# A 128-column score stationary, a refitted plan, finer weight loads and a cut-up last chunk in a fused attention and feed-forward kernel

## The chip, the cores and the metric

The kernel runs on one core of a Trainium2 chip. The metric is the device time of one execution in microseconds (us), median over runs; lower is better. Ratios are computed as the mean time of one kernel's runs over the mean of the other's from the same rounds, so they are not quite the ratio of the medians that I quote.

Some words used throughout. TensorE (PE in the profiles) multiplies a *stationary* operand, which is loaded into it first (such a load is a PEld line), by a *moving* one that streams through it. A *span* is the time from the first to the last instruction of one profiled execution; the *granted clock* is the share of full speed that TensorE was given. A *spell* is a stretch at half clock. The *scores* are q times k, and AV (`ps_av`) is their exponential times v. *Dead* or *warm-up* matmuls are run for the clock alone; nobody uses their results.

## The reference

Cosine attention for 8 batches of 12 heads (448 tokens of 64), followed by a multiplicative feed-forward layer:

```
q_n = q / (norm(q) + 1e-6);  k_n = k / (norm(k) + 1e-6)
attn = softmax(q_n @ k_n.T / tau);  x = (attn @ v), heads side by side      # 3584 x 768
out = ((x @ w1) * (x @ w2)) @ w3 @ w_out                                     # 768 -> 1024 -> 768
```

The kernel forms W34 = w3 @ w_out once (16 units of work on TensorE at the start) and applies it in place of both; a "W34 group" is one such unit. Heads are handled in 48 pairs, which come in groups of three.

## The kernel before

The order of all work on the five engines is fixed at build time by a small planner. Each step has engines with costs (in us), a rank, predecessors and buffers. The planner simulates and emits in that order; each engine then works through its own queue in order.

```python
def earliest(self, name, eng):                    # when could this step start on this engine
    st, t = self.steps[name], self.free[eng]
    for a in st["after"]:
        t = max(t, self.end[a] + (self.HOP + st["slack"] if self.where[a] != eng else 0.0))
    ...
ready = {n for n, k in left.items() if k == 0}    # a set: ties are broken in an order that
...                                               # differs from build to build
```

The scores of a pair, two heads at a time in the two halves of the rows, four chunks of 112 keys:

```python
for t in range(2):                                # t = 0: q, t = 1: k
    for j in range(NJ):
        nc.tensor.transpose(ps[:, t, j * P:(j + 1) * P], ..., ident[:P, :P])
...
nc.tensor.matmul(sc[:P, hh, :S],
                 qks[pp][64 * hh:64 * hh + 64, 1, c * P:(c + 1) * P],   # stationary, P = 112
                 qks[pp][64 * hh:64 * hh + 64, 0, :],                   # moving, 448 columns
                 start=True, stop=True)
```

The preparation of q and k per pair is a square, a sum (VectorE), a root (ScalarE) and a scaling; from the third group on, squares and scalings are GpSimd's alone. v is copied into a tile with a column of ones by GpSimd (`v_sb`). Loads and the last chunk:

```python
w3_part = [slice(k, k + 2) for k in range(0, KO2, 2)]          # w_out in two halves of 384 columns
loads = ["q0", "k0", "w30", "wo0", "v0", "w31", "q1", "k1", "w32",
         "w33", "v1", "wo1", "q2", "k2", "w10", "v2", "w20"]   # q0, k0: heads 2 to 5 of the first group
...
# last chunk of the output: two groups of 384 columns, each copied and stored on its own
for n in range(60):
    add(f"warm{n}", [("PE", ...)], 10000 + n, lambda e: warm(), ..., until=11.0)   # dead matmuls
```

Of the kernel before, what the change touches and what calls it, by code (L numbers as in the profile page):

```python
# [8 lines left out]
FP32 = mybir.dt.float32  # L9
# [10 lines left out]
class Plan:  # L20
# [23 lines left out]
    def add(self, name, on, rank, emit, after=(), takes=(), holds=(), kb=0, later=None,  # L44
            until=None, slack=0.0, port=False):
        self.steps[name] = dict(on=on, rank=rank, emit=emit, after=list(after), later=later,
                                takes=list(takes), kb=kb, until=until, slack=slack, port=port)
        for key in holds:
            self.holders.setdefault(key, []).append(name)
# [9 lines left out]
    def earliest(self, name, eng):  # L59
        st, t = self.steps[name], self.free[eng]  # L60
        for a in st["after"]:
            t = max(t, self.end[a] + (self.HOP + st["slack"] if self.where[a] != eng else 0.0))
        if st["later"]:
# [16 lines left out]
    def order(self):  # L80
# [7 lines left out]
        left = {n: len(need) for n, need in needs.items()}  # L88
        ready = {n for n, k in left.items() if k == 0}
        self.lanes, ring = [], self.RING_FREE  # L90
        self.port = dict(DVE=0.0, POOL=0.0)
        out = []
        while ready:
# [12 lines left out]
            st = steps[n]  # L106
            out.append((t, len(out), n, eng))
            ready.discard(n)
            self.start[n], self.free[eng] = t, t + cost
# [9 lines left out]
            for u in users.get(n, ()):  # L119
                left[u] -= 1  # L120
                if left[u] == 0:
                    ready.add(u)
        late = [n for n, st in steps.items() if n not in self.end and st["until"] is None]
# [5 lines left out]
def kernel(  # L129
# [133 lines left out]
    def tr(pp):  # L263
        g, i = divmod(pp, GP)
        n = nrms[g]
        ps = psT.tile([128, 2, 512], BF16, tag="tr", name="ps_tr")
        for t in range(2):
            for j in range(NJ):
                nc.tensor.transpose(  # L269
                    ps[:, t, j * P:(j + 1) * P],  # L270
                    n[:, i, t, j].rearrange("p h d -> p (h d)"),
                    ident[:P, :P])
        qks[pp] = head_pool.tile([128, 2, S], BF16, tag="qkT", name="qkT")
        pst[pp] = ps
# [4 lines left out]
    def scores(pp, half):  # L279
        if half == 0:  # L280
            exps[pp] = exp_pool.tile([P, NJ, 2, S], BF16, tag="exp", name="expT")
        for c in (2 * half, 2 * half + 1):
            sc = psS.tile([128, 2, 512], FP32, tag="sc", name="sc")
            for hh in range(2):
                nc.tensor.matmul(  # L285
                    sc[:P, hh, :S],
                    qks[pp][64 * hh:64 * hh + 64, 1, c * P:(c + 1) * P],
                    qks[pp][64 * hh:64 * hh + 64, 0, :],
                    start=True, stop=True)
            scs[pp, c] = sc  # L290
# [63 lines left out]

    def w34(fo, mh):
        ps = pms["w34", fo, mh] = psM.tile([128, 512], FP32, tag="pm", name="ps_w34")
        mm_group([(w3t_sb[:, go, fo * 128:(fo + 1) * 128],
                   wo_sb[:, go, mh * NH:(mh + 1) * NH]) for go in range(KO2)], ps[:, :NH])

    def w34_copy(fo, mh, eng):  # L360
        copy(eng, w34_sb[:, fo, mh * NH:(mh + 1) * NH], pms.pop(("w34", fo, mh))[:, :NH])

# [36 lines left out]

    def out_group(bb, ch, mh):  # L400
        ps = pms["o", bb, ch, mh] = psM.tile([128, 512], FP32, tag="pm", name="ps_o")
        mm_group([(abts[bb][:, fo, ch * 128:(ch + 1) * 128],
                   w34_sb[:, fo, mh * NH:(mh + 1) * NH]) for fo in range(KO2)], ps[:, :NH])

    def out_copy(bb, ch, mh, eng):
        if mh == 0:
            osbs[bb, ch] = opool.tile([128, DM], FP32, tag="out_sb", name="out_sb")
        copy(eng, osbs[bb, ch][:, mh * NH:(mh + 1) * NH], pms.pop(("o", bb, ch, mh))[:, :NH])
        if (bb, ch) == (B // 2 - 1, 2 * S // 128 - 1):
            store(bb, ch, osbs[bb, ch], slice(mh * NH, (mh + 1) * NH),  # L410
                  (nc.sync, nc.scalar) if mh else (nc.sync,))
        elif mh == 1:
            store(bb, ch, osbs.pop((bb, ch)), slice(None), (nc.sync,))
# [18 lines left out]
    def ones():  # L432
        for t in v_tiles:
# [8 lines left out]

    add("ident", [("POOL", 0.6)], -90, lambda e: make_identity(nc, ident), later="w30")
    add("ones", [("POOL", 0.45)], -70, lambda e: ones())
    every = slice(None)
    w3_part = [slice(k, k + 2) for k in range(0, KO2, 2)]
    weights = dict(w10=(w1_sb, moe_w1, every, every), w20=(w2_sb, moe_w2, every, every),
                   wo0=(wo_sb, moe_w_out, every, slice(0, NH)),
                   wo1=(wo_sb, moe_w_out, every, slice(NH, DM)))
    for n, part in enumerate(w3_part):  # L450
        weights[f"w3{n}"] = (w3_sb, moe_w3, part, every)
    loads = ["q0", "k0", "w30", "wo0", "v0", "w31", "q1", "k1", "w32",
             "w33", "v1", "wo1", "q2", "k2", "w10", "v2", "w20"]
    for g in range(3, NG):
        loads += [f"q{g}", f"k{g}", f"v{g}"]
    before = None
    for name in loads:
# [34 lines left out]
    for g in range(NG):  # L492
        for i in range(GP):
            p = g * GP + i
            for t in range(2):
# [4 lines left out]
                else:  # L500
# [9 lines left out]
                    slack=0.6 if g > 2 else 0.0)  # L510
                add(f"scale{p}.{t}", [("POOL", 1.04)] if g else [("DVE", 0.62)], p - 2,
                    lambda e, g=g, i=i, t=t: prep_scale(g, i, t, engines[e]),
# [17 lines left out]
    for p in range(NP):  # L530
        g, i = divmod(p, GP)
        b, blk = divmod(p, NPAIR)
        last = p > 0
        add(f"tr{p}", [("PE", 0.42)], p - 1.2, lambda e, p=p: tr(p),
            [f"scale{p}.0", f"scale{p}.1", "ident"] + ([f"tr{p - 1}"] if last else []),
# [4 lines left out]
        for h in range(2):  # L540
            add(f"sc{p}.{h}", [("PE", 0.6)], p + 0.5 * h - 1, lambda e, p=p, h=h: scores(p, h),
                [f"ev{p}"] + ([f"sc{p}.0"] if h else [f"sc{p - 1}.1"] if last else []),
# [6 lines left out]
        for h in range(2):  # L549
            add(f"av{p}.{h}", [("PE", 0.53)], p + 0.5 * h, lambda e, p=p, h=h: av(p, h),  # L550
                [f"exp{p}.{c}" for c in range(NJ)] + [f"spread{g}"]
# [4 lines left out]
                lambda e, p=p, h=h: av_norm(p, h), [f"av{p}.{h}"], holds=[("av", p, h)])  # L556
        add(f"tb{p}", [("PE", 0.24)], p + 1, lambda e, p=p: trback(p),
            [f"an{p}.0", f"an{p}.1"] + ([f"tb{p - 1}"] if last else []),
# [3 lines left out]

    line = []

    def fill(nm, cost, em, after, on, em2, takes=(), holds=(), after2=(), holds2=()):
        add(nm, [("PE", cost)], 1000 + len(line), em, after, [("pm", ("pm", nm))] + list(takes),
            holds, later=line[-1] if line else None)
        add(nm + ".c", on, -50, em2, [nm] + list(after2), holds=[("pm", nm)] + list(holds2))
        line.append(nm)

    def add_w3t(fo):
        fill(f"w3t{fo}", 0.46, lambda e: w3t(fo), ["ident", f"w3{fo // 2}"],
             [("DVE", 0.62), ("ACT", 0.95)], lambda e: w3t_copy(fo, e), holds=[("w3_sb",)])

    def add_w34(fo, mh):
        fill(f"w34.{fo}.{mh}", 1.3, lambda e: w34(fo, mh), [f"wo{mh}", f"w3t{fo}.c"],
             [("DVE", 0.5), ("ACT", 0.45)], lambda e: w34_copy(fo, mh, e))

    add_w3t(0)
    add_w3t(1)  # L580
    for fo in range(KO2):
        add_w34(fo, 0)
        if fo + 2 < KO2:
            add_w3t(fo + 2)
    for fo in range(KO2):
        add_w34(fo, 1)
    for b in range(B):
        bb = b // 2
        def add_a(fo):
            fill(f"a{b}.{fo}", 1.14, lambda e, b=b: a_group(b, fo),  # L590
                 [f"xt{b * NPAIR + i}" for i in range(NPAIR)] + ["w10"], [("ACT", 0.46)],
                 lambda e, b=b: a_copy(b, fo), [("a_sb", ("a_sb", b, fo))], [("xT", b)])

        def add_b(fo):
            fill(f"b{b}.{fo}", 1.14, lambda e, b=b: b_group(b, fo),
                 ["w20"], [("DVE", 0.55)], lambda e, b=b: b_mul(b, fo),
# [11 lines left out]
        for ch in (range(0, 3) if b % 2 == 0 else range(3, 7)):  # L608
            for mh in range(2):
                fill(f"o{bb}.{ch}.{mh}", 1.3, lambda e, bb=bb, ch=ch, mh=mh: out_group(bb, ch, mh),  # L610
                     [f"b{b}.{fo}.c" for fo in range(KO2)] + [f"w34.{KO2 - 1}.1.c"],
                     [("DVE", 0.5), ("ACT", 0.45)],
                     lambda e, bb=bb, ch=ch, mh=mh: out_copy(bb, ch, mh, e),
                     [] if mh else [("out_sb", ("out_sb", bb, ch))], [("big", bb)],
                     holds2=[("out_sb", bb, ch)] if mh else [])
    for n in range(60):
# [41 lines left out]
```

## Time and profile before

| | before |
|---|---|
| median, first three runs | 405.77 us (405.07 to 406.02) |
| span of the profiled run | 403.9 us, clock 1.000 |
| TensorE (PE) busy | 392.7 us, 97% |
| ScalarE (ACT), GpSimd (POOL), VectorE (DVE) | 61%, 61%, 54% |

TensorE is the bound; the question for each part of a change is whether it takes TensorE time away or removes a wait in front of TensorE. The lines are in the prediction.

### The profile page before, as it was taken

Reading aid. Unit: us, or ns where it says so; the run is one execution under the profiler, and the core shown is the slowest. Engines: PE = TensorE matmul, PEld = TensorE weight load, DVE = VectorE, ACT = ScalarE, POOL = GpSimd, SP = SyncE. Lnnn points to the kernel's source line nnn. Section 1 sums busy time; section 2 is a strip of 40 time slices with the busy share of each in tenths; the row PEclk is TensorE's granted clock in tenths of the full one; section 3 lists DMA queues with packets and bytes.
Section 4 is the critical chain, followed back from the end, with each engine's and each line's share of the span. In section 5 each row is a group of like instructions: output and inputs, shape, how many; then the busy total and the mean of one; then the engine's idle time right before and its main releaser. Section 6 shows DMA issues by size and latency. Waiting matters only on the chain.

```text
span 403.9 us, 9389 instructions
## 1 busy us (share of the span) xinstructions
PE 392.7 (97%) x3944; PEld 233.5 (58%) x3944; DVE 217.9 (54%) x487; ACT 246.0 (61%) x396; POOL 245.9 (61%) x258
## 2 busy tenths in 40 slices
PE   8799999999999999999999999999999999999995
PEld 4466565556555565556565565656655566555553
DVE  5686546595575765758657658444345443420210
ACT  5786677657676666656667658656656656423222
POOL 8479799999999999999999998515100000000000
PEclk9999999999999999999999999999999999999999
DMA  8999999265683484841945282200210013003005
GB/s 154 200 206 207 210 198 137 36 79 74 149 102 47 59 151 111 104 57 16 171 84 69 26 156 80 36 2 2 80 39 2 2 41 108 12 0 107 12 6 153
DMA packets 42475, 35.18 MB, mean 87 GB/s; under 512 B 1856, under 2 KB 36416, under 8 KB 42432
## 3 DMA queue, kind: packets, MB, share of 16 engines
q0 software_dynamic: 37312, 23.11, 41.5%
q1 hardware_dynamic: 4752, 11.07, 9.3%
q8 instruction: 31, 0.51, 0.5%
q10 hardware_dynamic: 368, 0.40, 0.3%
q14 instruction: 12, 0.10, 0.1%
HBM read 46.66 MB, written 11.01 MB: 143 GB/s over the span
## 4 chain that ended last, share of the span: by engine, by line
PE 80%; POOL 12%; DMA 4%; issue 2%; DVE 1%; ACT 0%; POOLq 0%
PE ps_b L337 17%; PE ps_a L337 17%; PE ps_o L337 16%; PE ps_av L302 11%; PE sc L285 10%; POOL nrm L256 4%; PE ps_tr L269 4%; DMA raw<-in_k_dram 4%; POOL sq L230 3%; PE ps_w L337 3%; PE ps_tb L324 3%; POOL raw L199 1%; POOL v_sb L215 1%; POOL vraw L206 1%; POOL w_sb L218 1%
## 5 line engine op out<-in xcount | busy, mean ns | idle before, releaser
L293 ACT ACTIVATE expT<-sc 112x896 bf16<-112x896 f32 x192 | 165.6, 915 | 54.0 <-PE sc L285 54.0
L337 PEld LDWEIGHTS <-w_sb 128*128 128x128 bf16 x768 | 69.4, 98 | 56.5 <-issue 4.0
L256 POOL TENSOR_TENSOR nrm<-raw,rn 112x512 bf16<-112x512 bf16 x90 | 90.8, 1035 | 4.3 <-PE ps_tr L269 2.1
L230 POOL TENSOR_TENSOR sq<-raw 112x512 bf16<-112x512 bf16 x87 | 87.7, 1038 | 0.2
L337 PE MATMUL ps_b<-xT,w_sb 128*128 128x448 bf16 x384 | 83.0, 353 | 0.0
L337 PE MATMUL ps_a<-xT,w_sb 128*128 128x448 bf16 x384 | 82.9, 353 | 0.0
L337 PE MATMUL ps_o<-w_sb,abT 128*128 128x384 bf16 x448 | 80.1, 327 | 0.0
L302 PEld LDWEIGHTS <-expT 112*128 112x128 bf16 x1536 | 59.6, 98 | 20.6 <-issue 9.0
L236 DVE TENSOR_REDUCE ss<-sq 112x8 f32<-112x512 bf16 x96 | 63.7, 679 | 12.6 <-POOL sq L230 10.1
L383 DVE TENSOR_TENSOR abT<-a_sb,ps_b 128x448 bf16<-128x448 bf16 x64 | 39.6, 619 | 53.8 <-PE ps_b L337 52.6
L302 PE MATMUL ps_av<-v_sb,expT 112*128 112x65 bf16 x1536 | 65.6, 195 | 1.7 <-POOL v_sb L215 1.1
L372 ACT CAST a_sb<-ps_a 128x448 bf16<-128x448 f32 x64 | 34.1, 533 | 40.0 <-PE ps_a L337 39.4
L285 PE MATMUL sc<-qkT 64*112 64x448 bf16 x384 | 56.6, 372 | 0.4 <-ACT expT L293 0.4
L337 PEld LDWEIGHTS <-abT 128*128 128x128 bf16 x448 | 41.3, 98 | 26.8 <-issue 3.0
L343 ACT COPY out_sb<-ps_o 128x384 f32<-128x384 f32 x39 | 18.7, 478 | 39.3 <-PE ps_o L337 37.6
L315 DVE TENSOR_TENSOR osd<-ps_av,rs 128x256 bf16<-128x256 f32 x96 | 40.8, 425 | 3.3
L314 DVE RECIPROCAL rs<-ps_av 128x4 f32<-128x4 f32 x96 | 17.2, 179 | 46.5 <-PE ps_av L302 46.1
L215 POOL COPY v_sb<-vraw 112x1536 bf16<-112x1536 bf16 x16 | 23.4, 1462 | 23.0 <-PE ps_av L302 23.0
L277 DVE COPY qkT<-ps_tr 128x896 bf16<-128x896 bf16 x48 | 29.8, 620 | 13.5 <-PE ps_tr L269 13.4
L331 DVE COPY xT<-ps_tb 128x448 bf16<-128x448 bf16 x48 | 18.6, 387 | 22.3 <-PE ps_tb L324 22.3
L269 PE MATMUL ps_tr<-ident,nrm 112*128 112x112 bf16 x384 | 27.3, 213 | 2.7 <-DVE nrm L256 1.2
L285 PEld LDWEIGHTS <-qkT 64*112 64x112 bf16 x384 | 17.4, 125 | 20.9 <-issue 17.6
(37 smaller groups left out, 213.9 us busy)
## 6 DMA issues: line engine op xcount, KB each, us to landing
vraw<-in_v_dram POOLq DMA_DIRECT2D x16, 336.0 KB, 4.9
raw<-in_q_dram POOLq DMA_DIRECT2D x15, 336.0 KB, 5.1
raw<-in_k_dram POOLq DMA_DIRECT2D x15, 336.0 KB, 7.4
w_sb<-in_moe_w_dram POOLq DMA_DIRECT2D x2, 1536.0 KB, 25.1
out_dram<-out_sb SPq DMA_DIRECT2D x7, 336.0 KB, 2.8
out_dram<-out_sb SPq DMA_DIRECT2D x8, 288.0 KB, 3.1
w_sb<-in_moe_w_dram POOLq DMA_DIRECT2D x4, 512.0 KB, 15.5
out_dram<-out_sb SPq DMA_DIRECT2D x8, 240.0 KB, 2.8
```

What stands on the lines that cost most here:

```text
L230: eng.tensor_mul(o, x, x)
L236: nc.vector.reduce_sum(sss[g][:, t, 2 * i:2 * i + 2, :], sqs.pop((g, i, t)), axis=AX.X)
L256: eng.tensor_mul(nrms[g][:, i, t].rearrange("p j h d -> p h j d"), raw_of(g, t, i), rns[g][:, t, 2 * i:2 * i + 2].to_broadcast([P, 2, NJ, D]))
L269: nc.tensor.transpose(ps[:, t, j * P:(j + 1) * P], n[:, i, t, j].rearrange("p h d -> p (h d)"), ident[:P, :P])
L277: nc.vector.tensor_copy(qks[pp], pst.pop(pp)[:, :, :S])
L285: nc.tensor.matmul(sc[:P, hh, :S], qks[pp][64 * hh:64 * hh + 64, 1, c * P:(c + 1) * P], qks[pp][64 * hh:64 * hh + 64, 0, :], start=True, s ...
L293: nc.scalar.activation(exps[pp][:, c], scs.pop((pp, c))[:P, :, :S], ACT.Exp, scale=1.0 / float(tau))
L302: nc.tensor.matmul(ps[:, m, :], exps[pp][:, c, hh, q0:q0 + 128], vt[:, 2 * i + hh, c, :], start=(c == 0), stop=(c == NJ - 1))
L315: nc.vector.tensor_mul(osds[pp][:, :, hh, :], ps[:, :, :D], rs.to_broadcast([128, NJ, D]))
L337: nc.tensor.matmul(o, l, r, start=(i == 0), stop=(i == len(pairs) - 1))
L372: nc.scalar.copy(a_sbs[b, fo], pms.pop(("a", b, fo))[:, :S])
L383: nc.vector.tensor_mul(abts[b // 2][:, fo, c0:c0 + S], a_sbs.pop((b, fo)), pms.pop(("b", b, fo))[:, :S])
```

## The change

Four things at once. The score stationary is read 128 columns wide. The planner's costs are refitted, ties are broken in a fixed order, a "lead" lets an output group start before its last product is ready, and scalings of the first group, but for its first pair, may go to GpSimd too. W3 comes in five parts and w_out in three, the first part of each at the head of the queue, and W34 groups follow their arrival. The last output chunk is cut into 384, 256 and 128 columns.

```diff
-                    ps[:, t, j * P:(j + 1) * P],
+                    ps[:, 1 - t, j * P:(j + 1) * P],
...
+                kq = qks[pp][64 * hh:64 * hh + 64].rearrange("p t s -> p (t s)")
                 nc.tensor.matmul(
-                    sc[:P, hh, :S],
-                    qks[pp][64 * hh:64 * hh + 64, 1, c * P:(c + 1) * P],
-                    qks[pp][64 * hh:64 * hh + 64, 0, :],
+                    sc[:, hh, :S], kq[:, c * P:c * P + 128], kq[:, S:],
                     start=True, stop=True)
...
-        ready = {n for n, k in left.items() if k == 0}
+        ready = {n: None for n, k in left.items() if k == 0}
...
-    w3_part = [slice(k, k + 2) for k in range(0, KO2, 2)]
+    w3_part = [slice(0, 1), slice(1, 2), slice(2, 4), slice(4, 6), slice(6, 8)]
+    wo_part = [slice(0, 192), slice(192, NH), slice(NH, DM)]
...
-    loads = ["q0", "k0", "w30", "wo0", "v0", "w31", "q1", "k1", "w32",
-             "w33", "v1", "wo1", "q2", "k2", "w10", "v2", "w20"]
+    loads = ["w30", "wo0", "q0", "k0", "w31", "v0", "w32", "q1", "k1", "wo1", "w33",
+             "w34", "v1", "q2", "wo2", "k2", "w10", "w20", "v2"]
...
-            add(f"sc{p}.{h}", [("PE", 0.6)], ...
+            add(f"sc{p}.{h}", [("PE", 0.58)], ...          # and six other costs, by 0.3 to 5%
...
+        edges = (0, NH, DM - 128, DM) if at_end(bb, ch) else (0, NH, DM)
```

## The prediction

> **What bounds the kernel now.** I first read the busy shares and the 40 slices of the page, then the table of windows, to see whether one engine sets the time and in which stretches it does not.
>
> ```profile
> PE 392.7 (97%) x3944; PEld 233.5 (58%) x3944; DVE 217.9 (54%) x487; ACT 246.0 (61%) x396; POOL 245.9 (61%) x258
> PE   8799999999999999999999999999999999999995
> PEclk9999999999999999999999999999999999999999
> ...
> 0.00:10.03 10.03, 8.77 (x38) 4.18 (x39) 4.99 (x11) 5.78 (x14) 8.74 (x19) 1.00 0.89 154
> 10.00:20.00 10.00, 7.19 (x85) 4.54 (x83) 6.78 (x13) 8.01 (x16) 4.49 (x5) 1.00 1.31 200
> 20.00:30.00 10.00, 9.50 (x122) 6.58 (x120) 8.38 (x20) 8.20 (x16) 7.25 (x9) 1.00 1.26 205
> 30.00:40.00 10.00, 9.34 (x115) 6.45 (x113) 6.15 (x14) 7.30 (x10) 9.68 (x11) 1.00 1.29 207
> 60.00:348.00 288.00, 286.53 (x3056) 170.84 (x3055) 170.57 (x390) 187.62 (x292) 198.42 (x199) 1.00 0.44 72
> ```
>
> Columns of a window: its length, then busy time (and instructions) of PE, PEld, DVE, ACT, POOL, clock, DMA share, GB/s. TensorE is the bound at full clock. Two stretches differ. Before 10.03 us its 38 instructions are warm-up matmuls whose results nobody uses (the first real one, a transpose, starts at 10.03), and from 10 to 40 us it waits while the DMA is at its highest, 200 GB/s. The last 4.2 us (399.7 to 403.9) are the last copy and store.
>
> Busy hides stalls, since a matmul's modelled end reaches past the start of the next. So I took start-to-start times of single matmuls from the trace: 189 ns at 448 columns, 162.5 at 384, 56 at 128, 49 at 112, 33 at 65. Laid against these, the real work from 10.03 to 399.54 is 381.5 us. TensorE loses beyond that 3.6 us in 10 to 20, 0.7 in 20 to 30, 1.0 in 30 to 40, 0.6 at 59, then 1.05 at 163.7 and 0.55 at 213.3 and otherwise about nothing. Account: 10.0 start + 0.4 stray warm-up + 7.5 lost + 381.5 + 4.35 tail = 403.8 of span 403.9. The timed median is 1.9 us more than the span.
>
> **What the scores cost.** A pair of timelines (start, length, instruction) and the forms of the weight loads:
>
> ```profile
> 253.04 0.59 PE L285 MATMUL sc<-qkT 64*112 64x448 bf16 x4
> 253.56 0.68 PE L302 MATMUL ps_av<-v_sb,expT 112*128 112x65 bf16 x16
> ...
> L285 PEld LDWEIGHTS <-qkT x4: 123/124/126, 270.7 to 270.7; 64*112 64x112 bf16 x4
> L285 PE MATMUL sc<-qkT x4: 349/372/393, 270.7 to 270.9; 64*112 64x448 bf16 x4
> ...
> L324 PE MATMUL ps_tb<-ident,osd x4: 220/220/231, 271.2 to 271.4; 128*128 128x128 bf16 x4
> ...
> L302 PEld LDWEIGHTS <-expT 112*128 112x128 bf16 x1536 | 59.6, 98 | 20.6 <-issue 9.0 <-ACT expT L293 0.8 <-DVE osd L315 0.8
> ```
>
> Four score matmuls are two pairs, each pair running together in the two halves of the rows. Two pairs at 189 ns are 378, but 253.04 to 253.56 is 520. In 96 of 96 groups the excess is the same: 93 ns on entry (448-column matmul to score 282 instead of 189, AV to score 123 to 124 instead of 33), 44 between the first and second pair (the first matmul of a group lasts 393 ns, the later one 349), 92 on leaving (281). Every other weight load of the kernel has 128 stationary columns, with 112 or 128 rows, and takes 98 ns; the scores' have 112 and take 123.
>
> **What the Trainium skill says.** "TensorE: Matmul & The Clock Gate", section "Weight-path perf modes — Fast Weight Load (FWL) and DoubleRow": fast load is on when the number of weights is 128 and the type is not FP32, and reads the weights as four chunks of 32 columns. The trace agrees: the 98 ns loads have a source pattern of 32 by 4, the 123 ns ones of 112 by 1. "TensorEngine Tiling (Array Packing)", "Key Properties": changing the tiling mode drains the engine. Consistent with the 93 and 92 ns, which I take to be the price of going to 64-row tiles and back; the change leaves it. "DMA: Bandwidth & Descriptors", "Specifications": under 512 B a transfer does read-modify-write. The 192-column parts of w_out land as 384 B runs; the kernel before has none of that size, so no run shows it yet.
>
> **Wide score stationary.** The stationary slice becomes 128 columns; columns 112 to 127 are other tokens (for the last chunk, q stored behind k, hence the swapped order of the transposes) and fill 16 output partitions that exp does not read. Matmul length stays 448 columns. The exposed part of a load that can't be hidden behind an earlier matmul is 44 ns for 112 columns. For 128 columns loaded fast it is 11 ns, seen where the transposes back follow a drain (231 against 220 ns). So a group should save 33 ns: 96 x 0.033 = 3.2 us. If the two fast loads of a pair can't run side by side, the second adds some 11 and it is 2.1. I take 2.8. It lies fully on the path, as TensorE loses nothing in most of 60 to 348 us. The plan's own costs agree in direction: 0.60 to 0.58 for scores. The other refitted costs (transposes 0.42 to 0.40) only reorder.
>
> **Finer loads at the start.** At 195 KB (as bf16) per us from 6 us on, with landing seen about 1.5 us after the last byte, the present order gives q0 7.1, k0 8.4, W3 part 0 11.0, wo0 15.1, v0 16.8, q1 21, k1 22.8, last W3 28, wo1 34. It reproduces the waits: q0 ends ACT's wait at 7.09, first W34 matmul at 14.95. On the same curve the new order gives W3 part 0 (half size) 7.3, wo0 (half size) 9.4, q0 10.5, k0 11.7, W3 13.1, v0 14.8, W3 17.4, q1 19.1, k1 20.9, wo1 22.8, W3 25.5 and 28.1, v1 29.8, wo2 35.5. What follows for TensorE:
> - One transpose group (0.45) and one W34 group (8 x 82 ns = 0.66) run before 10 us in place of warm-up: 1.1 us.
> - From 10 to 20 us: first pair 1.56, second pair's transposes and scores 1.56 (k0 is 3.3 us later, but this pair was waiting for ACT and DVE as much as for data), AV 1.05 (v0 is 2 us earlier, removing the 1.1 us wait for v_sb), one W3 row part 1.1, two more 2.2. Sum 7.5 of 10 against 6.0 now: 1.5 us.
> - From 20 to 40 us: W34 work of 6 us lands by 28 in place of waiting; perhaps 0.7 of the 1.7 lost is saved.
>
> Sum 3.3, as an upper guess, because the plan fixes TensorE's order in advance and a misjudged landing stalls it. I take 2.4. Against it: 16 groups of 192 columns cost 16 x 0.66 = 10.56 for 8 x 1.30 = 10.4, 0.15 us more.
>
> **Last chunk in pieces.** The last group of 384 columns (1.30) becomes 256 (8 x 109 = 0.87) and 128 (8 x 56 = 0.45): 0.02 more on TensorE. These rows end the kernel now:
>
> ```profile
> 399.74 0.48 ACT L343 COPY out_sb<-ps_o 128x384 f32<-128x384 f32 x1 [0.78 <-PE ps_o L337]
> 400.25 0.38 ACTq L396 DMA_DIRECT2D out_dram<-out_sb  x1
> ```
>
> The copy of 128 columns should take 0.25 to 0.28: 0.2 us. The store writes 112 runs of 512 B for 1536: its packets take 1.1 us now (401.1 to 402.2) and a third of that later, but the 256-column store is just ahead on the queue, so 0.3 to 0.5. Fixed parts (issue to first packet 0.85, end of program 1.2) stay. I take 0.5 in all. The "lead" lets the plan place an output group nearer the last product; TensorE loses nothing there now, so 0.
>
> **Mid-kernel stalls.** 1.8 us of single waits (59, 163.7, 213.3 us among them) depend on one order of work; a better fitted plan may have fewer. I take 0.4.
>
> **Sum.** 2.8 + 2.4 - 0.15 + 0.5 + 0.4 = 5.95: 405.77 - 6 = 399.8.
>
> **Rivals.** First, the drain hides the load: then 44 ns stays and the scores save nothing, about 402.6. For it: the drain dominates the excess; against it: the 393/349 and 231/220 differences, which are the loads alone. Second, the start gains nothing, as q0 and k0 come 3.3 us later and the W34 pieces (0.66 us of work per 384 KB, 2 us of DMA) can't fill TensorE: about 402.2; with slow 384 B runs another 1 to 2 us, 403.5. For it: the DMA runs at its limit until 60 us whatever the order. Against it: what is loaded first is now used first in small bites. Third, GpSimd, busy in 9 tenths of most slices until 250 us, takes over as the bound once TensorE needs less: its work per head pair is 2 squares and 2 scalings at 1.04, half a spread and a DMA issue, 5.4 us, against 7.2 us of TensorE per pair (345 / 48), so I give this under 1 us. Fourth, everything works, with 3.2 + 3.5 + 0.7 + 1.5 = 8.9: 396.9.
>
> **Range and chances.** Faster by over 2% means under 397.7, 8.1 us saved: it needs nearly the whole of the fourth case. I give it 0.17. Slower by 2% needs the start to go wrong by 14 us. Range 397.0 to 402.4; most likely 399.8.
>
> **What would show it.** Score loads of 98 ns; score matmuls of about 360 and 349 ns; score groups followed after 0.48 to 0.50 us instead of 0.52. First W3 transpose at about 7.5 us; TensorE busy over 8.5 us of 10 to 20. Last copy at or under 0.3 us, under 3.9 us from last matmul to the end. It would be wrong if the first score matmul still lasted 393 ns, if TensorE stood idle after 20 us for q1, k1 or v2 (now behind w20), or if new stalls over 0.5 us appeared after 60 us.

## The result and the profile after

| | before | after |
|---|---|---|
| median of 4 runs, same rounds | 405.89 us (405.07 to 406.10) | 401.00 us (400.63 to 401.97) |
| ratio, 95% interval | | 0.9887 (0.9865 to 0.9909) |
| span, mean clock of the profiled run | 403.9 us, 1.000 | 399.0 us, 0.995 |

The change saves about 1.1%. A second measurement with 6 runs against 11 of the kernel before gave 0.9907 (0.9879 to 0.9934).

The page of the changed kernel, busy shares and two rows of the 40 slices:

```profile
PE 389.2 (98%) x4006; PEld 231.5 (58%) x4006; DVE 218.2 (55%) x490; ACT 247.7 (62%) x402; POOL 247.2 (62%) x260
...
PE   8799999999999999999999999999999999999996
...
PEclk9899999999999999999999999999999999999999
```

TensorE is still the bound. New against the profile before is the 8 in the second slice of the clock row, where it was 9 throughout.

The windows of the changed kernel, with the columns as in the prediction (length, busy time of PE, PEld, DVE, ACT, POOL, clock, DMA share, GB/s):

```profile
0.00:10.03 10.03, 8.36 (x46) 4.33 (x47) 4.32 (x9) 3.93 (x11) 8.79 (x17) 1.00 1.03 165
10.00:20.00 10.00, 7.30 (x79) 5.12 (x77) 9.31 (x14) 8.49 (x18) 7.38 (x12) 0.83 1.35 199
20.00:30.00 10.00, 9.34 (x135) 7.71 (x132) 8.76 (x22) 8.78 (x20) 7.95 (x10) 1.00 1.29 204
30.00:40.00 10.00, 10.00 (x161) 8.09 (x157) 6.34 (x17) 7.40 (x11) 9.38 (x11) 1.00 1.25 209
60.00:348.00 288.00, 287.03 (x3100) 167.16 (x3099) 168.84 (x389) 192.83 (x298) 197.68 (x199) 1.00 0.44 71
```

From 30 us on nothing is missing until 60, and before 10 us there are now 22 real instructions among the warm-up. But 10 to 20 us is no fuller than before (7.30 against 7.19), at a granted clock of 0.83, with VectorE busy 9.31 of 10 us instead of 6.78.

I redid the account of the prediction for both traces: each start-to-start distance of two matmuls is compared with the usual one for its column count (189 ns at 448 columns and so on), and what is over it counts as lost. The first row holds the 1.26 us before the first instruction and all dead matmuls.

| us | before | after | difference |
|---|---|---|---|
| before the first instruction, and warm-up | 10.42 | 9.86 | -0.56 |
| lost between 10 and 60 us | 6.00 | 5.43 | -0.57 |
| lost after 60 us | 1.93 | 1.54 | -0.39 |
| real work | 381.03 | 378.11 | -2.92 |
| last matmul's start to the end of the span | 4.52 | 4.09 | -0.43 |
| span | 403.90 | 399.03 | -4.87 |

So of 4.9 us, 2.9 are work, mostly the scores; the start gives 1.1, the stalls after 60 us and the tail 0.4 each. A score group of the changed kernel (least, median and longest ns, then first and last start):

```profile
L287 PEld LDWEIGHTS <-qkT x4: 93/94/96, 271.6 to 271.6; 64*128 64x128 bf16 x4
L287 PE MATMUL sc<-qkT x4: 349/354/360, 271.6 to 271.8; 64*128 64x448 bf16 x4
```

The load is recorded with 94 ns in place of 124, and the first matmul of a group with 360 in place of 393. In the 96 groups the second pair now starts 200 ns after the first (it was 233; medians); the entry rose from 93 to 96 ns, and leaving stayed at 92 to 93. That is some 31 ns per group, 3.0 us in all.

The end of the changed kernel (start, length, instruction):

```profile
395.15 0.34 ACTq L396 DMA_DIRECT2D out_dram<-out_sb  x1
395.53 0.27 ACT L343 COPY out_sb<-ps_o 128x128 f32<-128x128 f32 x1 [0.41 <-PE ps_o L337]
395.82 0.37 ACTq L396 DMA_DIRECT2D out_dram<-out_sb  x1
```

The last copy takes 0.27 us for 0.48, as worked out. But it starts 0.37 us after the modelled end of the last matmul (395.16), where the kernel before needed 0.04 (399.71 to 399.74): in between, ScalarE's queue issues the store of the 256-column piece (395.15 to 395.49). The profile names TensorE as what the copy waited for, but by these times the store's issue is in the way. It takes back 0.33 us of what the tail could have won; no run tests this.

TensorE's queue where the clock fell (start, length, and the idle time before with what ended it):

```profile
11.37 0.55 PE L287 MATMUL sc<-qkT 64*128 64x448 bf16 x4
11.85 0.62 PE L350 MATMUL ps_w<-ident,w_sb 128*128 128x128 bf16 x8
13.98 0.83 PE L337 MATMUL ps_w<-wo_sb,w3t_sb 128*128 128x192 bf16 x8 [1.51 <-DVE w3t_sb L345]
14.75 0.55 PE L287 MATMUL sc<-qkT 64*128 64x448 bf16 x4
16.44 1.16 PE L270 MATMUL ps_tr<-ident,nrm 112*128 112x112 bf16 x8 [1.14 <-DVE nrm L257]
17.39 1.91 PE L350 MATMUL ps_w<-ident,w_sb 128*128 128x128 bf16 x16
```

W3's second part is there early, and its transposes run at 11.85, but VectorE copies them out only after four sums, so the W34 group waits 1.5 us. The second pair's transposes wait another 1.1 us for VectorE's scaling. Then eight transposes take 1.16 us and sixteen take 1.91, about twice what they took elsewhere: the clock was at half from 16.08 to 19.49 us.

### The profile page after: what moved, and what is told of

The parts are those of the page before. It is cut to its first block, busy times and chain, and to the rows that moved or that the text cites. A ratio compares the mean times of both kernels' runs of the same rounds, so it can differ in the third digit from the quotient of the medians.

```text
span 399.0 us, 9513 instructions
## 1 busy us (share of the span) xinstructions
PE 389.2 (98%) x4006; PEld 231.5 (58%) x4006; DVE 218.2 (55%) x490; ACT 247.7 (62%) x402; POOL 247.2 (62%) x260
## 4 chain that ended last, share of the span: by engine, by line
PE 74%; POOL 19%; DVE 3%; issue 2%; ACT 0%; ACTq 0%; POOLq 0%; DVEq 0%
PE ps_b L337 15%; PE ps_a L337 15%; PE ps_o L337 14%; PE ps_av L302 10%; PE sc L287 8%; POOL sq L231 8%; POOL nrm L257 8%; PE ps_w L337 5%; PE ps_tr L270 4%; PE ps_tb L324 2%; POOL v_sb L216 2%; PE ps_warm L437 2%; POOL raw L200 2%; DVE ss L237 1%; PE ps_w L350 1%
## 5 line engine op out<-in xcount | busy, mean ns | idle before, releaser
L337 PEld LDWEIGHTS <-w_sb 128*128 128x128 bf16 x768 | 71.0, 98 | 60.3 <-issue 3.0
L337 PE MATMUL ps_o<-w_sb,abT 128*128 128x384 bf16 (+2 forms) x456 | 79.9, 323 | 0.0
L302 PEld LDWEIGHTS <-expT 112*128 112x128 bf16 x1536 | 58.1, 98 | 19.0 <-issue 11.5
L287 PE MATMUL sc<-qkT 64*128 64x448 bf16 x384 | 53.0, 354 | 0.0
L343 ACT COPY out_sb<-ps_o 128x384 f32<-128x384 f32 (+2 forms) x46 | 21.7, 471 | 40.1 <-PE ps_o L337 39.5
L270 PEld LDWEIGHTS <-nrm 112*128 112x128 bf16 x384 | 20.5, 98 | 13.6 <-issue 7.4
```

The lines of the kernel that those rows point to most:

```text
L270: nc.tensor.transpose(ps[:, 1 - t, j * P:(j + 1) * P], n[:, i, t, j].rearrange("p h d -> p (h d)"), ident[:P, :P])
L287: nc.tensor.matmul(sc[:, hh, :S], kq[:, c * P:c * P + 128], kq[:, S:], start=True, stop=True)
L302: nc.tensor.matmul(ps[:, m, :], exps[pp][:, c, hh, q0:q0 + 128], vt[:, 2 * i + hh, c, :], start=(c == 0), stop=(c == NJ - 1))
L337: nc.tensor.matmul(o, l, r, start=(i == 0), stop=(i == len(pairs) - 1))
```

## The experiments

Twelve kernels ran, in three calls of four; six runs of each, four of runs 9 and 12. The kernel before had medians of 404.72, 404.81 and 404.90 us in them (11 runs each). I built the kernel before twice more: the instructions stood in another order each time, since the planner's set is walked in another order in each build. So "before" is one draw among several orders, and most experiments start from the changed kernel, whose order is reproducible.

**1. Narrow stationary in the changed kernel** (label narrow). The edit takes back the first two hunks of the diff and nothing else.

```diff
-                    sc[:, hh, :S], kq[:, c * P:c * P + 128], kq[:, S:],
+                    sc[:P, hh, :S], qks[pp][64 * hh:64 * hh + 64, 1, c * P:(c + 1) * P],
+                    qks[pp][64 * hh:64 * hh + 64, 0, :],
```

> The changed kernel with the score stationary back at 112 columns; the order of work is the same instruction for instruction. Theory: a group of scores loses 35 ns between its first and second pair and gains 3 ns on entry, so the wide stationary is worth 96 x 0.032 = 3.1 us and this kernel takes 401.0 + 3.1 = 404.1 us (ratio to the kernel before 0.995 to 0.997). Rival: the drain hides the load and the gain of the change comes from the new order of work alone; then this takes 401.0 to 401.6 us.

Measured: 402.62 us (401.64 to 403.65), ratio 0.994. That lies between the two theories: 1.3 to 1.6 us over the changed kernel (401.31 in the next call, 401.00 in the first), not the 3.1 of the theory. These medians come from different calls; by the ratios to the kernel before it is 1.3 to 2.1 us, so the size rests on the account of the traces more than on them. The score work is there in full (49.9 against 46.6 us without the entries), but the time lost after 60 us is 0 instead of 1.5 us. With the wide stationary, TensorE runs into waits that it does not have when it is slower. The window from 160 to 240 us, first of the changed kernel, then of this run:

```profile
160.00:240.00 80.00, 79.03 (x892) 45.70 (x891) 53.42 (x121) 58.07 (x92) 76.92 (x79) 1.00 0.54 77
```

```profile
160.00:240.00 80.00, 80.00 (x900) 47.78 (x898) 54.28 (x122) 58.83 (x93) 76.92 (x78) 1.00 0.54 77
```

PE is the second number: 79.03 against 80.00. POOL, the sixth, is 76.9 of 80 in both: GpSimd is at its limit there. How such a wait reaches TensorE, in the changed kernel at 164 us (other instructions between these are left out):

```profile
164.14 0.69 DVE L237 TENSOR_REDUCE ss<-sq 112x8 f32<-112x512 bf16 x1 [1.70 <-POOL sq L231]
165.29 0.61 DVE L278 COPY qkT<-ps_tr 128x896 bf16<-128x896 bf16 x1
165.96 0.38 PE L324 MATMUL ps_tb<-ident,osd 128*128 128x128 bf16 x4 [0.42 <-DVE qkT L278]
```

VectorE waits 1.70 us for a square of GpSimd's; the copy `qkT`, behind that sum in its queue, comes late; and TensorE waits for that copy. Run 8 tests it.

**2. Old loads in the changed kernel** (label loads_old). W3 in four parts, w_out in two, the old queue and the old order of W34 groups.

```diff
-    w3_part = [slice(0, 1), slice(1, 2), slice(2, 4), slice(4, 6), slice(6, 8)]
-    wo_part = [slice(0, 192), slice(192, NH), slice(NH, DM)]
-    loads = ["w30", "wo0", "q0", "k0", "w31", "v0", ...]
+    w3_part = [slice(k, k + 2) for k in range(0, KO2, 2)]
+    wo_part = [slice(0, NH), slice(NH, DM)]
+    loads = ["q0", "k0", "w30", "wo0", "v0", "w31", ...]
```

> The changed kernel with the loads and the W34 groups of the kernel before (four parts of W3, two of w_out, old order), all else kept. Theory: the finer loads win 1.2 us net in the first 60 us, because a spell at half the TensorE clock near 16 to 19.5 us costs some 1.6 us of what they could win; so this takes 402 to 402.5 us, with the clock full from 5 us to the end. Rival 1: the half clock costs as much as the loads win, 400.5 to 401.3. Rival 2: the loads are worth the 2.4 us that the prediction gave them and the half clock comes from elsewhere, 403.4 with the clock still falling.

Measured: 401.61 us (401.25 to 403.29), ratio 0.9917, clock 1.000 in five of six runs. This is just under the theory's 402 and just above rival 1. The finer loads are worth little, 0.3 to 0.6 us by the medians of neighbouring calls, which is within the noise.

**3. Old tail in the changed kernel** (label tail_old).

```diff
-        edges = (0, NH, DM - 128, DM) if at_end(bb, ch) else (0, NH, DM)
+        edges = (0, NH, DM)
```

> The changed kernel with the last output chunk in two halves of 384 columns as before. Theory: the piece of 128 columns saves 0.2 us of copy and 0.25 us of store, so this takes 401.45 us and its span from the last matmul to the end is 4.45 us instead of 4.04. Rival: the last store queues behind the one before it and nothing is saved, 401.0.

Measured: 401.34 us (400.88 to 401.63), ratio 0.9904. The median cannot tell 0.4 us, since the changed kernel itself spread over 400.0 to 402.8. The trace can: from the start of the last matmul to the end of the span it is 4.50 us, against 4.09 with the pieces. The difference of 0.41 is the one expected (the expectation counted to a point 0.05 us before the end).

**4. The kernel before with a fixed order of ties** (label before_fixed).

```diff
-        ready = {n for n, k in left.items() if k == 0}
+        ready = {n: None for n, k in left.items() if k == 0}
```

> The kernel before with one thing of the change: ready steps kept in order of entry instead of in a set, so that ties are broken the same way in each build (two builds of the kernel before differ in their order of work). Theory: the order of ties is luck of a microsecond at most, 405 to 407 us. Rival: a good part of the change is this fixed order, then 403 to 404.5 us.

Measured: 404.70 us (404.22 to 405.31), ratio 0.9988 (0.9966 to 1.001). The fixed order by itself is worth nothing that these runs can show.

**5. The changed kernel unaltered** (label after_again), as the yardstick.

> The changed kernel unaltered, as the yardstick for the other runs of this call. All theories: 401 us within 1 us, the clock at half for some 3.4 us near 16 us, and single waits of 1.3 us in sum between 160 and 240 us.

Measured: 401.31 us (400.03 to 402.81), ratio 0.9907. The waits after 60 us are there again (1.5 us), but this profiled run had no spell at half clock, and its span is 398.0 instead of 399.0 us. So whether a spell comes is luck of the single execution.

**6. The idle spells filled with dead matmuls** (label clock_kept).

```diff
     for n, e in plan.order():
+        if n in ("w34.1.0", "tr1"):
+            ps = psM.tile([128, 512], FP32, tag="pm", name="ps_keep")
+            for _ in range(7 if n == "w34.1.0" else 5):
+                nc.tensor.matmul(ps[:, :S], warm_sb[:, :128], warm_sb[:, :S], start=True, stop=True)
```

> The changed kernel with 7 dead matmuls put before the second W34 group and 5 before the second pair's transposes, where TensorE stood idle for 1.5 and 1.2 us; the order of all else is kept. Theory: the idle spell from 12.5 to 16.4 us is what drops the clock to half; with it filled the clock stays full and the work from 16.4 to 19.9 us takes 1.6 us less, so 1 to 1.6 us less than the unaltered kernel. Rival: the half clock falls in time that is waited for anyway (data, v, DVE), and the total moves by less than 0.4 us although the clock stays full.

Measured: 399.95 us (399.58 to 400.84), ratio 0.9874, against 401.31 for the unaltered kernel. The mean clock is at least 0.998 in all six runs; the spread fell from 2.8 to 1.3 us. The dead matmuls and what follows them in TensorE's queue:

```profile
13.48 1.49 PE L642 MATMUL ps_keep<-warm_sb 128*128 128x448 bf16 x7
15.02 0.82 PE L337 MATMUL ps_w<-wo_sb,w3t_sb 128*128 128x192 bf16 x8
15.78 0.55 PE L287 MATMUL sc<-qkT 64*128 64x448 bf16 x4
16.26 1.12 PE L642 MATMUL ps_keep<-warm_sb 128*128 128x448 bf16 x5
17.22 0.82 PE L270 MATMUL ps_tr<-ident,nrm 112*128 112x112 bf16 x8
17.93 1.05 PE L350 MATMUL ps_w<-ident,w_sb 128*128 128x128 bf16 x16
```

The same sixteen transposes take 1.05 us here instead of 1.91. The gain of 1.4 us is in the range expected. Still, the two intervals overlap (0.985 to 0.9897 and 0.9879 to 0.9934), and this profiled run's span, 398.7, is above the lucky one of the yardstick; in it, a W3 part landed later (a wait of 0.75 us). So it is a likely gain, in that the bad executions vanish, and not a proven one.

**7. v's copy held back** (label gate). In the trace of the changed kernel one scaling on VectorE took 2.54 us while GpSimd copied v beside it. Here GpSimd's copy waits for that pair's second scaling.

```diff
+    steps.insert(at["scale1.1"], s0)                 # s0: the copy of v, moved behind it
     ...
+        if n == "spread0":
+            nc.gpsimd.tensor_copy(gate_sb, nrms[0][:, 1, 1, NJ - 1, 1, D - 1:])
```

> The changed kernel with GpSimd's first copy of v held back until VectorE's second scaling of the second pair is done (a one-element copy on GpSimd reads its result); the order on the other engines is kept. Theory: that scaling took 2.54 us instead of 0.68 because GpSimd's v copy ran beside it; apart, both scalings take 0.7 us, the second pair's transposes start about 1.1 us earlier (15.3 instead of 16.4 us), the clock may then stay full, and the total falls by 0.7 to 2.5 us. Rival: the scaling is slow for another reason and still takes over 2 us, or what follows waits for exp and v in any case; total within 0.4 us.

Measured: 400.74 us (400.11 to 401.46), ratio 0.9891: 0.6 us less than the yardstick, within the overlap of the intervals. The second pair's transposes began at 15.92 us instead of 16.44, half of the 1.1 us expected. The mechanism is shown, the worth is not. The scalings of the changed kernel, then of this run (least, median, longest):

```profile
L257 DVE TENSOR_TENSOR nrm<-raw,rn x4: 672/674/2536, 13.8 to 18.3; 112x512 bf16<-112x512 bf16 x4
```

```profile
L257 DVE TENSOR_TENSOR nrm<-raw,rn x3: 681/684/1906, 13.9 to 15.5; 112x512 bf16<-112x512 bf16 x3
```

Both scalings of the second pair took 0.68 us, but now the next pair's, which began at 15.49 us beside the moved copy (15.39 to 16.86), took 1.91. The delay went wherever the copy went. The Trainium skill, "SBUF — State Buffer", section "SBUF: two separate sides", says that a VectorE operation with two SBUF inputs and a GpSimd operation that reads SBUF exclude each other for a whole instruction; these traces agree: the slow scaling ended 0.55 us after the end of GpSimd's copy in the changed kernel (16.38 and 15.83) and 0.54 us after it in this run (17.40 and 16.86). The page also says that whichever starts first goes first; the records do not show that, since in the changed kernel the scaling had started 0.50 us before the copy. The profiled run also had a spell at half clock, so the clock did not stay full.

**8. One square in six on ScalarE** (label sq_act).

```diff
+        if n[:2] == "sq" and n[-2:] == ".1" and int(n[2:-2]) % GP == 2 and int(n[2:-2]) > 2 * GP:
+            e = "ACT"
```

> The changed kernel with one of the six squares of each group of three pairs moved from GpSimd to ScalarE from the third group on; order kept. Theory: the 1.5 us of waits between 160 and 240 us come from GpSimd, which VectorE's sums wait for with evictions queued behind them; with 1.04 us less per group of 16.5 us on GpSimd they vanish and the total falls by 1.2 to 1.5 us. Rival: exp on ScalarE is delayed by the extra squares and the waits only change place; total within 0.5 us or higher.

Measured: 400.40 us (399.01 to 401.61), ratio 0.9879, 0.9 us less than the yardstick; span of the profiled run 396.9 against 398.0. The waits are gone:

```profile
160.00:240.00 80.00, 80.00 (x914) 46.97 (x916) 54.84 (x124) 61.82 (x98) 72.91 (x74) 1.00 0.57 80
```

GpSimd is down from 76.9 to 72.9 us and TensorE is full at 80.00. The time lost after 60 us is 0.05 instead of 1.5 us. The median alone, at this spread, would not prove it; the trace shows that the waits went, and so do those of runs 9 and 12, which have the same edit.

**9. Both mends together** (label clock_sq): the edits of 6 and 8.

> The changed kernel with both mends: the 12 dead matmuls in TensorE's idle spells near 13 and 15 us, and one square in six on ScalarE from the third group on. Theory: the two act in different stretches and add up, so 1.3 + 1.0 us under the unaltered kernel: 398.7 to 399.2 us, ratio to the kernel before about 0.985, no waits over 0.2 us between 60 and 348 us. Rival: they share a cause and only one counts, 399.9 us or more.

Measured: 399.36 us (399.25 to 399.68), ratio 0.9855 (0.9827 to 0.9883). The gain is a little less than the expected sum. All four runs are faster than any of the kernel before and of the changed one (400.03 the fastest, in another call). No wait over 0.1 us is left from 60 to 348 us:

```profile
60.00:348.00 288.00, 288.00 (x3109) 168.18 (x3109) 169.48 (x389) 199.77 (x312) 185.70 (x186) 1.00 0.44 72
```

**10. The same, narrow** (label clock_sq_narrow): the edit of 1 on top of 9.

> The same with the score stationary at 112 columns, order kept. Theory: without the waits on GpSimd the wide stationary has its whole worth, 96 x 0.032 to 0.035 = 3.1 to 3.4 us, so this takes 3.1 to 3.4 us more than the run before it in this call (402 us); in the unaltered kernel half of it was given back as waits. Rival: the waits had nothing to do with it and the difference stays at 1.6 us.

Measured: 402.24 us (401.42 to 402.42), ratio 0.9921. The difference to run 9 in the same rounds is 2.9 us, and the two ranges are far apart. With GpSimd relieved and the clock full, the wide stationary is worth nearly all of the 3.0 us of its matmuls; in the changed kernel as it stands about half of that came back as waits (1.5 us in its traces).

**11. Wide stationary alone** (label before_wide): the fixed order of 4 and the first two hunks of the diff.

> The kernel before with the fixed order of ties and the wide score stationary, nothing else; its instructions stand in the same order as in the run with the fixed order alone (404.7 us). Theory: the matmul work falls by 3.1 us, of which up to 1.5 us may come back as waits on GpSimd between 160 and 240 us, so 401.6 to 403.1 us. Rival: the wide stationary is worth its 3.1 us only together with the fitted plan, 404 us or more.

Measured: 403.82 us (403.27 to 405.39), ratio 0.9969, against 0.9988 for run 4. I had expected 401.6 to 403.1, and the rival 404 or more; it is 0.9 us better than run 4, with overlapping intervals, and no more. The score groups shortened as in the changed kernel (233 to 200 ns), but the time lost after 60 us rose from 1.5 to 3.3 us. TensorE's longest waits in this run (total, times, longest):

```profile
PE ps_tr L269 <- DVE nrm L256: 2.0, 3, 1.0
PE ps_av L301 <- DVE osd L314: 1.5, 3, 0.7
```

In run 4 there was one wait for `osd`, of 0.5 us; in the kernel before, none. With the costs of the old plan, the order seems no longer to suit the faster scores; no run tests that reading.

**12. Old loads with the square moved** (label loads_old_sq): the edits of 2 and 8.

> The changed kernel with the old loads and W34 order, and one square in six on ScalarE; its clock is full without dead matmuls. Against the first run of this call it shows what the finer loads are worth once the clock is kept: theory 1.4 to 2 us more, 400.4 to 400.9 us; rival: the loads are worth under 0.7 us even then, 399.4 us or less.

Measured: 399.74 us (399.68 to 399.96), ratio 0.9865, against 399.36 for run 9 in the same rounds. The rival holds as to size: the finer loads are worth 0.4 us, even with the clock kept. (Run 9 has the dead matmuls and run 12 has not, so what these cost by themselves is in the 0.4. Run 8, which has the finer loads and no dead matmuls, took 399.01 and 399.61 us in its two executions at clock 1.000.) The account shows where the rest went. Run 9 does 1.0 us of real work before 10 us and run 12 0.1; from 10 to 20 us it is 5.0 (without dead matmuls) against 6.7; from 20 to 60 us 39.1 against 38.2. What the weights win by coming first, q0 and k0 lose by coming later.

**The clock, over all traces.** I looked at twelve of the traces (before, after, and all runs but two of the last call) for when the clock falls. After it has become full, every change of it that the traces show lies a whole number of steps of 3.41 us from that moment (in the changed kernel full at 5.84, then changes after 3, 4 and 115 steps, at 16.08, 19.49 and 398.37 us); so I take it to be judged in such steps. While there was work it fell four times, once in each of the traces of after, narrow, tail_old and gate, and in the step before each fall TensorE had been busy for 1.32, 1.19, 1.32 and 1.40 us, with modelled ends. In every other step of the first 24 us of all twelve traces it was busy for 1.70 us or more, and the clock stayed. The two remaining traces have no step under 2.28 us before the end. The two steps of the changed kernel around its fall:

```profile
12.67:16.08 3.41, 1.32 (x12) 0.72 (x12) 3.41 (x4) 3.22 (x11) 2.69 (x4) 1.00 1.21 205
16.08:19.49 3.41, 3.00 (x31) 2.77 (x32) 3.06 (x7) 2.09 (x4) 1.67 (x2) 0.50 1.49 195
```

Where the steps lie differs from trace to trace (the clock became full between 4.0 and 6.7 us), and in the unaltered kernel's second trace the emptiest step held 1.70. This fits that the same program has a spell in one execution and none in another. The Trainium skill, "TensorE: Matmul & The Clock Gate", Part 1, describes this free-running window of about 3.4 us; the length agrees.

What a spell costs is less sure. In the fourteen traces a mean clock of 0.996 or less goes with a spell and one of 0.998 or more with none. By that mark the kernel before had spells too, in some executions (its slowest, 407.03 and 407.10 us, have 0.993 and 0.994), and its first profile caught one without. And the unaltered changed kernel took 400.03, 401.02 and 401.31 us in its executions of run 5 without a spell, 401.32 to 402.81 in those with; run 8 took 399.01 and 399.61 without, 400.32 to 401.61 with; but run 7 took 400.19 to 401.46 without and 400.11 and 400.92 with. A spell tends to cost about 1 us, and no run isolates it.

## Why the prediction was right or wrong

The time was right: 401.0 for 399.8, within 397.0 to 402.4, a saving of 4.9 us for the 6.0 predicted. Of the five terms of the sum, two hold (the 0.15 us for narrower W34 groups and, nearly, the last chunk), one holds only under a condition, one was far too large, and one came out by accident.

- **TensorE as the bound** holds before and after, and nothing else took over as a whole.
- **Wide stationary, 2.8 us.** The mechanism was right and so was the size per group: 33 ns between the pairs (233 to 200), as predicted. The second load of a pair costs 3 ns on entry, not the 11 that I feared. The rival of the drain hiding the load is out. What failed is "It lies fully on the path": that is true only with GpSimd relieved (2.9 us, runs 9 and 10), while in the changed kernel 1.3 to 2.1 us arrived, by how the calls are compared (1.5 us came back as waits in its traces), and in the old plan 0.9.
- **GpSimd as the third rival**, "under 1 us", is what took the difference: 1.5 us of waits after 60 us (runs 1 and 8). I compared its 5.4 us per pair with TensorE's average of 7.2. But the planner runs attention ahead at GpSimd's pace: in the window from 160 to 240 us it is busy 76.9 of 80. An average over the kernel hid it. The wait shows as one for VectorE, whose sums wait for GpSimd's squares with evictions behind them in the queue. One of the prediction's own signs of being wrong thus came true: the trace has new stalls over 0.5 us after 60 us (0.6 at 166 and 0.7 at 204 us, start to start).
- **Finer loads, 2.4 less 0.15.** This term was mis-sized: 0.4 us (runs 9 and 12). The landing times were right (first W3 transposes at 7.67 us, predicted about 7.5), and so was the work before 10 us (1.4 us between two traces, 1.1 predicted). The step that failed is the list for 10 to 20 us with "Sum 7.5 of 10"; TensorE was busy for 7.30 us there, not over 8.5. It counted work whose data had landed and forgot the engine that passes it on. VectorE was busy 9.31 of 10 us there (1.9 of it in the scaling that GpSimd's v copy held up), so TensorE waited 1.5 us for the W3 copy and 1.1 us for that scaling. Real work in that stretch was 4.4 us (5.4 in the trace without the spell), less than the 6.0 of before. The spell at half clock, which the prediction did not think of, came on top: the two profiled runs of the same program have spans of 399.0 with it and 398.0 without, though executions without it also reached 399.1 and 399.4.
- **The last chunk, 0.5**, measured 0.4 in the traces, from the last matmul's start; 0.1 of that is only that this matmul is shorter (128 columns). The copy gave the 0.2 predicted, and from its store's issue to the end it is 3.21 us for 3.65; what spoiled it is the 0.33 us that the copy started late, behind the extra store on its queue. The sign "under 3.9 us from last matmul to the end" failed: 4.1.
- **Mid-kernel stalls, 0.4**, came out at 0.39, but not for the reason given. The fitted order has none at all with narrow scores (run 1); with wide ones it has new ones.
- **What it left out:** the order of the kernel before differs from build to build. That did not matter in the end (run 4).
- **Two slips in its working** changed nothing: the single waits from 59 us on add up to 2.2 us in its own account, not 1.8, and GpSimd's share of v per pair is a third of a copy, not half.

That the sum came out near is luck in part, because the errors went both ways. The predicted terms were 1.9 us too high for the loads and some 1 to 1.5 too high for the scores as delivered, and the refitted plan, to which I gave nothing by itself, made up for part of it. Between run 11 and run 2, which share wide scores and old loads, lie 2.2 us (in different calls), of which 0.4 are the tail; the rest is the fitted costs, the lead and the freedom to scale the first group on GpSimd. I did not separate these three.

## What to carry to other kernels

When the bound engine gets faster, look at the suppliers in the stretch where they are busiest, not at their average: here one engine at 62% of the span stood at 96% where it counted, and moving a sixth of one operation off it took away the waits behind it. Data that lands early is worth only as much as the engine between it and the bound engine has room. And if the fixed order of work comes from a planner, break its ties reproducibly before comparing, and refit its costs together with each change of speed.

## What the Trainium skill lacked or had wrong

- "TensorE: Matmul & The Clock Gate", Part 1 and the table of advice: the page speaks of an idle window and of gaps over some 3 us, and of one kernel with frequent short idle spells, without a share. Here steps of 3.41 us with TensorE busy for 1.19 to 1.40 us (35 to 41%), with no single wait over 1.7 us in the changed kernel, were enough for the half clock, and 1.70 us (50%) were not.
- The same page, "LDWEIGHTS": columns over 1.2 would be 93 ns for 112 columns. The exposed part in these traces was 44 ns for 112 columns (233 less 189) and 11 for 128 loaded fast (200 less 189), in records of 123 and 94 ns.
- "TensorEngine Tiling (Array Packing)", "Key Properties": that a change of mode drains the array is said without a size. The traces show 93 to 96 ns on the way in and 92 to 93 on the way out, for switching between full rows and 64-row tiles, whatever the load.
- "DMA: Bandwidth & Descriptors", "Specifications": the read-modify-write under 512 B did not show as a slower load. With 768 KB of w_out landing in runs of 384 B (4.7 to 21.8 us), the DMA moved 199 GB/s from 10 to 20 us, against 200 before; a packet of 384 B took 51 ns, one of 512 B 60 and one of 768 B 79 (medians), which is a line without a step at 512 B.
